# The second batch's split three units later in the dense layers, and the three products of a unit in another order

## The chip, the cores and the metric

One core of a Trainium2 chip. The metric is the time of one execution on the device in microseconds (us). Three runs of the kernel before took 1726.03, 1732.5 and 1733.97 us, median 1732.5.

## The reference, cut to what matters

```python
# x, v: (2, 12480, 128) f32
h_filt = (np.maximum(pos_emb @ w1, 0) @ w2) * np.exp(-0.01 * pos)[:, None]
y = irfft(rfft(x * v, n=2 * S, axis=1) * rfft(h_filt, n=2 * S, axis=0), n=2 * S, axis=1)[:, :S]
a = (x * y).reshape(24960, 128)              # a long convolution, gated by x
h = a @ w_in                                 # (24960, 2048)
g = np.maximum(h, 0) + alpha * np.minimum(h, 0)
out = (g @ w_out).astype(np.float32)         # (24960, 128)
```

## The kernel before, in words

The first third of the execution (to about 607 us) transforms the inputs and leaves the product of the spectra in DRAM (`g_d`). The change does not touch it. The rest is `phase_b`: the last stage of the inverse transform, the gate with x, and the two dense layers.

`phase_b` works in 32 **passes** (`k`, `NK = 32`). A pass covers 390 tokens of each of the two batches and walks over the 2048 hidden columns in 16 **units** (`f`, `NFT = 16`) of 128 columns. Numbers are kept in two fp16 halves, a high and a low one, so a product of two numbers is three matmuls: high by high, high by low, low by high. `mm3` (L1180) issues them, each for both batches, six matmuls a unit and layer.

The units overlap. In each step of the loop `for n in range(total + LAG)` (L1294) the program writes down, in this order:

- `layer1(n)`: six matmuls from the pass's input halves `ah` and `alo` into a PSUM tile `hp`, of which there are two in turn; ScalarE (ACT) takes `Relu(-h)` out of it (L1262), and VectorE (DVE) makes the activation from both (L1263, the op named `ring<-ring,keep,hp`). So unit n cannot start its matmuls before the L1263 of unit n-2 is done.
- `halve(n-1)`: ACT rounds the activation to fp16 (`g_hi`, L1269), and the rest (`g_lo`, L1270) is taken by DVE for even units, by GpSimd (POOL) for odd ones.
- `layer2(n-4)` (`LAG = 4`): six matmuls from `g_hi` and `g_lo` into `o`, the pass's output.
- one or two **steps of the next pass**, by a table that gives the step numbers for each unit: step 1 and 2 split the spectra of the first and the second batch into halves (`gh` on ACT, L1144, and `gl` on POOL, L1145); 3 and 5 are the last transform of either batch, 24 small matmuls into `yp` (L278 to L280); 4 and 6 the gate (DVE, L284); 7 the squares for the norm (ACT, L1160, and a cast on DVE); 8 their sum over partitions (one matmul, L1164); 9 the scales (five tiny DVE ops); 10 the halves `ah` (ACT, L1174) and `alo` (DVE, L1175) with which unit 0 of the next pass begins.

Each engine runs its instructions in the order in which they are written down; nothing reorders them. The table `usual` (L1292) holds for passes 1 to 30. Pass 0 has a table of its own, `late`, since its inputs come late, and pass 31 has no next pass to prepare. `late` has step 9 at unit 13 and step 10 at unit 14.

Of the kernel before, what the change touches and what calls it, by code (L numbers as in the profile page):

```python
# [49 lines left out]
LAG = 4  # L50
# [69 lines left out]
class Plan:  # L120
# [7 lines left out]
    LAG = {"PE": 200, "ACT": 150, "DVE": 110, "POOL": 110, "DMA": 1700, None: 0}  # L128
# [159 lines left out]
def body(ctx, tc, A, out, stop=None, dbg=None):  # L288
# [815 lines left out]
    with tc.manual_schedule():  # L1104
        ve.memset(ones, 1.0)
        ve.memset(one1, 1.0)
        with ExitStack() as ctx_a:
            xt = phase_a()
        if stop in ("p", "r"):
            return  # L1110
        if stop == "a":
            sy.dma_start(out=dbg["g"], in_=g_d)
            sy.dma_start(out=dbg["iu"], in_=s_u)
            sy.dma_start(out=dbg["ih"], in_=s_h)
            return
        phase_b(ctx, tc, A, out, locals())


def phase_b(ctx, tc, A, out, v):
# [58 lines left out]
        return st, norm, total, power, halves  # L1178

    def mm3(o, wh, wl, dh, dl, start, stop, bs=range(B)):  # L1180
        for n, (w, d) in enumerate(((wh, dh), (wh, dl), (wl, dh))):
            for b in bs:
                te.matmul(o[:, b, :TOK], w, d[:, b], start=start and n == 0, stop=stop and n == 2)  # L1183

# [52 lines left out]
    for n in range(NFT // 4):  # L1237
        c = n == 0 and FIRST
        w = sb.tile([128, 4 - c, 4, 128], F16, tag=f"w{n}", bufs=1, name="w")
# [15 lines left out]
    def layer1(n, d):  # L1255

        f = n % NFT
        hp = ps.tile([128, 2, 512], F32, tag="h", name="hp")
        mm3(hp, wt[0, f], wt[1, f], d["h"], d["l"], True, True)
        h = hp[:, :, :TOK]  # L1260
        neg, acts[n] = slot(n % 3), slot(3 + n % 3)
        ac.activation(neg, h, AF.Relu, scale=-1.0)  # L1262
        ve.scalar_tensor_tensor(out=acts[n], in0=neg, scalar=keep[:, f:f + 1], in1=h, op0=ALU.mult, op1=ALU.add)  # L1263
# [9 lines left out]
    def layer2(n):  # L1273
        k, f = divmod(n, NFT)
        if f == 0:
            outs[k] = ps.tile([128, 2, 512], F32, tag="o", bufs=1, name="o")
        d = parts.pop(n)
        split = n == total - 1
        for bs in [(b,) for b in range(B)] if split else [range(B)]:
            mm3(outs[k], wt[2, f], wt[3, f], *d, f == 0, f == NFT - 1, bs)  # L1280
        if f == NFT - 1:
            ot = sb.tile([D, B, TOK], F32, tag="ot", name="ot")
            for b in range(B):
                ac.activation(ot[:, b], outs[k][:, b, :TOK], AF.Copy, scale=backs[k][:, b:b + 1])  # L1284
                if split:
                    (sy, ac)[b].dma_start(out=out[k][:, b], in_=ot[:, b])
            if not split:
                sy.dma_start(out=out[k], in_=ot)
            outs.pop(k)


    usual = {0: [1], 2: [2], LAG: [3], LAG + 1: [4], 7: [5], 8: [6], 9: [7], 11: [8], 12: [9], 13: [10]}  # L1292
    late = {4: [1], 5: [2], 7: [3], 8: [4], 9: [5], 10: [6], 11: [7], 13: [8, 9], 14: [10]}
    for n in range(total + LAG):  # L1294
        k, f = divmod(n, NFT)
        if n < total:
            if f == 0:
                d = st["a"]
# [72 lines left out]
```

## Time and profile before

| | |
|---|---|
| median of three runs | 1732.5 us |
| the profiled execution, its own time | 1733.39 us |
| its span in the trace | 1731.5 us |
| PE (matmul) busy | 1616.6 us, 93% of the span |
| DVE busy | 1399.2 us, 81% |
| ACT busy | 1341.1 us, 77% |
| POOL busy | 968.8 us, 56% |
| dense layers, matmuls L1183 | from 612.6 us to the end |

The shares are means over both parts of the program. Times in the trace are counted from the start of the span. In a timeline a row is one instruction, or several alike in a row (x2); what stands in brackets is how long the engine was idle before it, and on whose result it waited.

### The profile page before, as it was taken

The page shows a single profiled execution, that of the slowest core. Times are in us where ns is not written, and L with a number is a line of the kernel's source. Part 1 is how long each engine was busy: PE and PEld are TensorE (multiplying, and loading weights), DVE is VectorE, ACT ScalarE, POOL GpSimd, SP SyncE. Part 2 cuts the span into 40 slices and gives each one's busy share as a digit, 9 for nine tenths or more (in the row PEclk, how much of TensorE's full clock was granted, in tenths as well). Part 3 has the DMA queues.
Part 4 walks back from the last instruction along what each step waited for, and adds up shares of the span by engine and source line. Part 5 has one row for each costly group of instructions (what it writes and reads, how often), then busy time and mean ns, then how long its engine had stood idle before and what let it go on. Part 6 is the DMA issues. An engine that isn't in the chain of part 4 may idle for free.

```text
span 1731.5 us, 34059 instructions
## 1 busy us (share of the span) xinstructions
PE 1616.6 (93%) x13260; PEld 1146.1 (66%) x13260; DVE 1399.2 (81%) x1931; ACT 1341.1 (77%) x2218; POOL 968.8 (56%) x687
## 2 busy tenths in 40 slices
PE   6988888888888989999999999999999999999998
PEld 4987877887778945665566556655665556555655
DVE  6566899986988778888888888888888888888886
ACT  6456677676786578888888888888888888888886
POOL 5356689777687145545554555445544554455443
PEclk8776898998999999999999999999999999999999
DMA  7142243675442960220221202202112022021100
GB/s 209 62 143 99 92 141 129 193 230 180 152 147 85 251 160 20 72 54 20 53 58 34 53 19 72 54 20 53 54 38 53 20 72 54 19 54 51 41 10 19
DMA packets 95568, 144.59 MB, mean 84 GB/s; under 512 B 7187, under 2 KB 63861, under 8 KB 93967
## 3 DMA queue, kind: packets, MB, share of 16 engines
q1 hardware_dynamic: 94287, 141.72, 28.0%
q8 instruction: 103, 1.69, 0.4%
q10 hardware_dynamic: 1120, 0.70, 0.1%
q14 instruction: 58, 0.48, 0.1%
HBM read 100.39 MB, written 42.01 MB: 82 GB/s over the span
## 4 chain that ended last, share of the span: by engine, by line
PE 62%; DVE 16%; ACT 9%; issue 6%; DMA 5%; POOL 2%; SPq 0%; POOLq 0%; ACTq 0%; DVEq 0%
PE hp L1183 24%; PE o L1183 22%; DVE ring L1263 4%; DVE ring L828 4%; PE mm L430 3%; ACT ring L1262 3%; DVE ring L838 3%; DMA g_d<-ring 2%; DMA first<-in_xv 2%; ACT g_hi L1269 2%; POOL ring L679 1%; PE yp L278 1%; PE yp L279 1%; PE yp L280 1%; DVE g_lo L1270 1%
## 5 line engine op out<-in xcount | busy, mean ns | idle before, releaser
L1183 PEld LDWEIGHTS <-w 128*128 128x128 f16 x6144 | 590.1, 97 | 444.0 <-issue 35.2
L1270 POOL TENSOR_TENSOR g_lo<-ring,g_hi 128x780 f16<-128x780 f32 x256 | 442.3, 1728 | 546.3 <-ACT g_hi L1269 546.2
L1263 DVE SCALAR_TENSOR_TENSOR ring<-ring,keep,hp 128x780 f32<-128x780 f32 x512 | 524.3, 1024 | 188.2 <-ACT ring L1262 181.4
L1262 ACT ACTIVATE ring<-hp 128x780 f32<-128x780 f32 x512 | 419.1, 819 | 169.1 <-PE hp L1183 167.6
L1183 PE MATMUL hp<-ah,w 128*128 128x390 f16 x2048 | 506.0, 328 | 15.1 <-DVE ring L1263 14.1
L1183 PE MATMUL o<-g_hi,w 128*128 128x390 f16 x2048 | 504.4, 328 | 0.7 <-ACT ot L1284 0.7
L1269 ACT ACTIVATE g_hi<-ring 128x780 f16<-128x780 f32 x512 | 433.8, 847 | 2.6 <-DVE ring L1263 0.3
L1270 DVE TENSOR_TENSOR g_lo<-ring,g_hi 128x780 f16<-128x780 f32 x256 | 330.4, 1291 | 0.0
L1183 PE MATMUL hp<-alo,w 128*128 128x390 f16 x1024 | 253.4, 328 | 0.8 <-DVE alo L1175 0.8
L1183 PE MATMUL o<-g_lo,w 128*128 128x390 f16 x1024 | 252.6, 328 | 0.6 <-POOL g_lo L1270 0.6
L1145 POOL TENSOR_TENSOR gl<-gt,gh 90x1024 f16<-90x1024 f32 x62 | 132.7, 2141 | 0.0
L828 DVE TENSOR_TENSOR ring<-mm,ring 128x512 f32<-128x512 f32 (+2 forms) x188 | 116.1, 657 | 17.3 <-ACT ring L816 16.4
L855 POOL TENSOR_TENSOR z<-ring,z 128x512 f16<-128x512 f32 x88 | 110.5, 1256 | 7.2 <-ACT z L851 7.2
L729 DVE TENSOR_TENSOR z<-mm,z 128x720 f16<-128x720 f32 (+1 forms) x99 | 85.6, 878 | 31.2 <-ACT z L726 31.1
L929 PE MATMUL mm<-t,z 128*128 128x128 f16 x512 | 102.5, 232 | 7.9 <-ACT z L851 3.8
L833 POOL TENSOR_TENSOR ring<-ring 128x256 f32<-128x256 f32 (+1 forms) x90 | 80.7, 897 | 48.1 <-DVE ring L828 39.8
L714 PE MATMUL mm<-t,ring 98*128 98x180 f16 (+1 forms) x320 | 83.5, 264 | 20.5 <-DVE z L729 5.3
L931 PE MATMUL mm<-t,z 128*128 128x128 f16 x512 | 101.8, 231 | 0.1
L930 PE MATMUL mm<-t,z 128*128 128x128 f16 x512 | 101.8, 231 | 0.0
L679 POOL TENSOR_TENSOR ring<-ring 98x512 f16<-98x512 f32 x63 | 78.9, 1267 | 39.0 <-ACT ring L676 25.5
L726 ACT ACTIVATE z<-mm 128x720 f16<-128x720 f32 (+1 forms) x99 | 74.4, 757 | 31.7 <-PE mm L716 31.1
L946 DVE TENSOR_TENSOR ring<-mm,ring 90x504 f32<-90x504 f32 (+2 forms) x132 | 80.5, 656 | 21.6 <-ACT ring L943 20.3
(177 smaller groups left out, 2939.4 us busy)
## 6 DMA issues: line engine op xcount, KB each, us to landing
g_d<-ring SPq DMA_DIRECT2D x32, 720.0 KB
gt<-g_d SPq DMA_DIRECT2D x16, 1440.0 KB
ring<-in_tw SPq DMA_DIRECT2D x34, 512.0 KB
ring<-in_xv SPq DMA_DIRECT2D x72, 196.0 KB
xt<-in_xt SPq DMA_DIRECT2D x31, 390.0 KB
out_t<-ot SPq DMA_DIRECT2D x31, 390.0 KB
first<-in_xv SPq DMA_DIRECT2D x56, 196.0 KB
first<-in_tw SPq DMA_DIRECT2D x12, 512.0 KB
```

Of the source, the lines that this page charges most:

```text
L679: either[e].tensor_tensor(out=halves(h)[:, 1], in0=xr(j), in1=halves(h)[:, 0], op=ALU.subtract)
L828: ve.tensor_tensor(out=t[:, :, m], in0=p[:, :, m], in1=hs[:, a:a + 1, m].to_broadcast([128, 2, (b1 - b0) * 2 * ZC]), op=ALU.mult)
L855: e.tensor_tensor(out=zl, in0=v, in1=zh, op=ALU.subtract)
L929: te.matmul(o, hi, t3[:, 0], start=True, stop=False)
L930: te.matmul(o, hi, t3[:, 1], start=False, stop=False)
L931: te.matmul(o, lo, t3[:, 0], start=False, stop=True)
L1145: po.tensor_tensor(out=dl, in0=src, in1=dh, op=ALU.subtract)
L1183: te.matmul(o[:, b, :TOK], w, d[:, b], start=start and n == 0, stop=stop and n == 2)
L1262: ac.activation(neg, h, AF.Relu, scale=-1.0)
L1263: ve.scalar_tensor_tensor(out=acts[n], in0=neg, scalar=keep[:, f:f + 1], in1=h, op0=ALU.mult, op1=ALU.add)
L1269: ac.activation(gh, a, AF.Copy)
L1270: (ve, po)[n % 2].tensor_tensor(out=gl, in0=a, in1=gh, op=ALU.subtract)
```

## The change

Two edits. In `mm3` the three products of a unit come in the order high by high, low weight by high data, high weight by low data; before, the product with the low data came second. `mm3` serves both layers. In the table `usual`, step 2 (the second batch's split) moves from unit 2 to unit 5, and steps 5 to 10 each move one unit later. The same instructions are issued, in equal numbers.

```diff
     def mm3(o, wh, wl, dh, dl, start, stop, bs=range(B)):
-        for n, (w, d) in enumerate(((wh, dh), (wh, dl), (wl, dh))):
+        for n, (w, d) in enumerate(((wh, dh), (wl, dh), (wh, dl))):
             for b in bs:
                 te.matmul(o[:, b, :TOK], w, d[:, b], start=start and n == 0, stop=stop and n == 2)
...
-    usual = {0: [1], 2: [2], LAG: [3], LAG + 1: [4], 7: [5], 8: [6], 9: [7], 11: [8], 12: [9], 13: [10]}
+    usual = {0: [1], LAG: [3], LAG + 1: [4, 2], 8: [5], 9: [6], 10: [7], 12: [8], 13: [9], 14: [10]}
     late = {4: [1], 5: [2], 7: [3], 8: [4], 9: [5], 10: [6], 11: [7], 13: [8, 9], 14: [10]}
```

The end of a pass on DVE, before: L1263 of unit 12, the five tiny ops of step 9 (L332 to L1170), L1263 of unit 13, `g_lo` of unit 12, the two `alo`, L1263 of units 14 and 15, and `g_lo` of unit 14.

```order
L1263 SCALAR_TENSOR_TENSOR ring<-ring,keep,hp 128x780
L332 TENSOR_SCALAR yp<-yp 128x2
L333 TENSOR_SCALAR yp<-yp 128x2
L334 TENSOR_SCALAR kap<-yp 128x2
L338 TENSOR_SCALAR yp<-kap 128x2
L1170 TENSOR_SCALAR osc<-yp,igsc 128x2
L1263 SCALAR_TENSOR_TENSOR ring<-ring,keep,hp 128x780
L1270 TENSOR_TENSOR g_lo<-ring,g_hi 128x780
L1175 SCALAR_TENSOR_TENSOR alo<-a,kap,ah 128x390 x2
L1263 SCALAR_TENSOR_TENSOR ring<-ring,keep,hp 128x780 x2
L1270 TENSOR_TENSOR g_lo<-ring,g_hi 128x780
```

The same place on DVE with the change: L1263 of units 12 and 13, `g_lo` of unit 12, the tiny ops, L1263 of unit 14, the two `alo`, L1263 of unit 15, `g_lo` of unit 14.

```order
L1263 SCALAR_TENSOR_TENSOR ring<-ring,keep,hp 128x780 x2
L1270 TENSOR_TENSOR g_lo<-ring,g_hi 128x780
L332 TENSOR_SCALAR yp<-yp 128x2
L333 TENSOR_SCALAR yp<-yp 128x2
L334 TENSOR_SCALAR kap<-yp 128x2
L338 TENSOR_SCALAR yp<-kap 128x2
L1170 TENSOR_SCALAR osc<-yp,igsc 128x2
L1263 SCALAR_TENSOR_TENSOR ring<-ring,keep,hp 128x780
L1175 SCALAR_TENSOR_TENSOR alo<-a,kap,ah 128x390 x2
L1263 SCALAR_TENSOR_TENSOR ring<-ring,keep,hp 128x780
L1270 TENSOR_TENSOR g_lo<-ring,g_hi 128x780
```

The tiny ops now stand behind the `g_lo` of unit 12, and the two `alo` stand behind the L1263 of unit 14 where they stood ahead of it.

The start of a pass on POOL, before: the seven odd `g_lo` that end with that of unit 15, the first batch's `gl`, `g_lo` of unit 1, the second batch's `gl`, the seven `g_lo` of units 3 to 15.

```order
L1270 TENSOR_TENSOR g_lo<-ring,g_hi 128x780 x7
L1145 TENSOR_TENSOR gl<-gt,gh 90x1024
L1270 TENSOR_TENSOR g_lo<-ring,g_hi 128x780
L1145 TENSOR_TENSOR gl<-gt,gh 90x1024
L1270 TENSOR_TENSOR g_lo<-ring,g_hi 128x780 x7
```

The same place on POOL with the change:

```order
L1270 TENSOR_TENSOR g_lo<-ring,g_hi 128x780 x6
L1145 TENSOR_TENSOR gl<-gt,gh 90x1024
L1270 TENSOR_TENSOR g_lo<-ring,g_hi 128x780 x2
L1145 TENSOR_TENSOR gl<-gt,gh 90x1024
L1270 TENSOR_TENSOR g_lo<-ring,g_hi 128x780 x6
```

The second `gl` has moved behind the `g_lo` of unit 3; the first one stands where it stood.

## Rows read from the trace of the kernel before

**Rows 1.** The page, busy time of each engine, its share of the span, instructions.

```profile
PE 1616.6 (93%) x13260; PEld 1146.1 (66%) x13260; DVE 1399.2 (81%) x1931; ACT 1341.1 (77%) x2218; POOL 968.8 (56%) x687
```

**Rows 2.** Busy time by window, passes 1 to 30: length, engines, clock, DMA.

```profile
660.00:1700.00 1040.00, 1027.17 (x7206) 620.95 (x7205) 864.31 (x1021) 881.18 (x1258) 535.54 (x298) 1.00 0.16 44
```

**Rows 3.** Waits from 640 to 1700 us: total us, times, longest.

```profile
PE hp L1183 <- DVE ring L1263: 12.6, 32, 0.4
PE hp L1183 <- DVE alo L1175: 0.8, 2, 0.6
```

**Rows 4.** Timeline of PE in an ordinary pass; unit 0 at 857.08.

```profile
839.96 0.21 PE L278 MATMUL yp<-t,gh 90*128 90x98 f16 x1
...
849.01 0.49 PE L1183 MATMUL hp<-ah,w 128*128 128x390 f16 x2
...
856.64 0.49 PE L1183 MATMUL o<-g_hi,w 128*128 128x390 f16 x2
857.08 0.49 PE L1183 MATMUL hp<-ah,w 128*128 128x390 f16 x2
...
864.71 0.49 PE L1183 MATMUL o<-g_hi,w 128*128 128x390 f16 x2
865.61 0.49 PE L1183 MATMUL hp<-ah,w 128*128 128x390 f16 x2 [0.40 <-DVE ring L1263]
```

**Rows 5.** Timeline of DVE in the same stretch.

```profile
837.03 0.96 DVE L1270 TENSOR_TENSOR g_lo<-ring,g_hi 128x780 f16<-128x780 f32 x1
...
838.45 1.02 DVE L1263 SCALAR_TENSOR_TENSOR ring<-ring,keep,hp 128x780 f32<-128x780 f32 x1
...
847.76 1.03 DVE L1263 SCALAR_TENSOR_TENSOR ring<-ring,keep,hp 128x780 f32<-128x780 f32 x1 [0.65 <-ACT ring L1262]
...
854.93 1.16 DVE L1175 SCALAR_TENSOR_TENSOR alo<-a,kap,ah 128x390 f16<-128x390 f32 x2
856.00 2.12 DVE L1263 SCALAR_TENSOR_TENSOR ring<-ring,keep,hp 128x780 f32<-128x780 f32 x2
...
862.52 2.10 DVE L1270 TENSOR_TENSOR g_lo<-ring,g_hi 128x780 f16<-128x780 f32 x1
864.54 2.04 DVE L1263 SCALAR_TENSOR_TENSOR ring<-ring,keep,hp 128x780 f32<-128x780 f32 x2
```

**Rows 6.** Timeline of ACT in the same stretch.

```profile
835.95 0.85 ACT L1269 ACTIVATE g_hi<-ring 128x780 f16<-128x780 f32 x1
...
859.79 1.05 ACT L1144 ACTIVATE gh<-gt 90x1024 f16<-90x1024 f32 x1
```

**Rows 7.** Timeline of POOL in the same stretch.

```profile
861.66 2.13 POOL L1145 TENSOR_TENSOR gl<-gt,gh 90x1024 f16<-90x1024 f32 x1
```

**Rows 8.** Timeline of PE where pass 1 begins, after pass 0's table `late`.

```profile
647.26 0.49 PE L1183 MATMUL o<-g_hi,w 128*128 128x390 f16 x2
647.60 0.49 PE L1183 MATMUL hp<-ah,w 128*128 128x390 f16 x2
648.66 0.33 PE L1183 MATMUL hp<-alo,w 128*128 128x390 f16 x1 [0.57 <-DVE alo L1175]
649.20 0.33 PE L1183 MATMUL hp<-alo,w 128*128 128x390 f16 x1 [0.21 <-DVE alo L1175]
649.36 0.49 PE L1183 MATMUL hp<-ah,w 128*128 128x390 f16 x2
649.69 0.49 PE L1183 MATMUL o<-g_hi,w 128*128 128x390 f16 x2
```

**Rows 9.** Timeline of DVE at that place.

```profile
646.50 1.02 DVE L1263 SCALAR_TENSOR_TENSOR ring<-ring,keep,hp 128x780 f32<-128x780 f32 x1
647.43 1.71 DVE L1175 SCALAR_TENSOR_TENSOR alo<-a,kap,ah 128x390 f16<-128x390 f32 x2
649.06 1.01 DVE L1263 SCALAR_TENSOR_TENSOR ring<-ring,keep,hp 128x780 f32<-128x780 f32 x1
```

**Rows 10.** Timeline of POOL at that place.

```profile
646.51 1.67 POOL L1270 TENSOR_TENSOR g_lo<-ring,g_hi 128x780 f16<-128x780 f32 x1 [1.69 <-ACT g_hi L1269]
```

## The prediction

> **What bounds the kernel now.** I read the page first: PE is busy 93% of the span, DVE 81%, ACT 77% [rows 1]. That is a mean over two unlike parts, so the second view is the busy time of the dense layers alone: in the 1040 us from 660 to 1700 PE is busy 1027.17 us at the full granted clock, DVE 864, ACT 881, POOL 536 [rows 2]. The stretch that the change touches is bound by matmuls, and all that can be won or lost there is a wait of PE. The third view lists those waits: PE waits for DVE's L1263 32 times, 12.6 us in all, and twice for `alo`, 0.8 us [rows 3]. The fourth, the timeline of PE, places them. Matmuls in an unbroken stream start 0.166 us apart, a pair of them 0.33 us (649.36 to 649.69, [rows 8]), so a pair that comes later than 0.33 us after the one before it shows a loss:
>
> - Unit 4: the pair at 864.71 should be followed at 865.04 and is followed at 865.61 [rows 4]. 0.57 us lost, in each of passes 1 to 30.
> - Unit 0: 856.64 is followed at 857.08 [rows 4], 0.44 where 0.33 is due. 0.11 us lost in each of passes 2 to 31.
>
> So a pass loses 0.68 us, 30 passes 20 us. No rearrangement of this kind can win more than these 20 us, and it can lose more.
>
> **What holds unit 4.** It needs the PSUM tile of unit 2, so the L1263 of unit 2. That one starts at 864.54 (the first of the x2 there) and takes 1.02 us: 865.56, then PE at 865.61 [rows 4, 5]. DVE was late with it because the `g_lo` of unit 0 ahead of it ran from 862.52 to 864.62, 2.10 us where the same op takes 0.96 us elsewhere in the pass (837.03) [rows 5]. Beside it POOL ran a `gl` from 861.66 to 863.79 [rows 7]: 863.79 + 0.96 = 864.75, so the DVE op did next to nothing until POOL was done. Which `gl`? The ACT op that feeds it is the `gh` at 859.79 [rows 6], in unit 0: it belongs to the first batch. The change leaves step 1 in unit 0. The second batch's `gl`, which does move, comes behind the `g_lo` of unit 1 on POOL and so after 863.79, when unit 4's fate is already decided. So I cost the removal of the second split from unit 2 at nothing: it frees DVE and ACT in units 3 and 4, and PE shows no wait there after 865.61 that could go. The 0.57 us stay.
>
> **What holds unit 0, and what the later steps do to it.** Before, the two `alo` run at 854.93 to 856.09, one whole unit before unit 0 needs them; the 0.11 us come from L1263 of unit 14, which they push to 856.00 + 1.02 = 857.02 [rows 4, 5]. With the change the tiny ops of step 9 stand at unit 13 and the `alo` at unit 14, behind the L1263 of that unit. This order exists in the trace already: the table `late` of pass 0 has steps 9 and 10 at the same units. There L1263 of unit 14 starts at 646.50, the two `alo` start at 647.43 and end at 649.14, 1.71 us for both instead of 1.16 [rows 5, 9]. The extra 0.55 us stands beside POOL's `g_lo` of unit 13, 646.51 to 648.18 [rows 10]; in the ordinary pass no such overlap falls on `alo`. PE starts the next pass's unit 0 on time at 647.60, but has its `alo` products only at 648.66 and 649.20, and layer 2 follows at 649.69 [rows 8]: 2.09 us for a unit of six matmuls that takes 1.00 us. 1.09 us lost.
>
> Each boundary of passes 1 to 30 should now look like that one: POOL's `g_lo` of unit 13 hangs on ACT and PE, and DVE's queue from `g_lo` of unit 12 to `alo` is the same in both. Step 8 comes one unit earlier than in `late`, which changes nothing, since in pass 0 DVE goes on to the tiny ops without a pause.
>
> The new order of products eases it. Four of the six matmuls now need only `ah`: they start at 647.60 to 648.10, the fifth would start at 648.26 and waits for 648.66, the sixth for 649.20, and layer 2 starts at 649.36. That is 649.36 - 647.60 - 1.00 = 0.76 us lost instead of 1.09.
>
> The Trainium skill, "SBUF — State Buffer", section "Who interferes with whom", says that a DVE op with two SBUF inputs and a GpSimd op that reads SBUF exclude each other, and that the second to issue is blocked until the first has finished. That agrees in kind with the rows. Taken to the letter, `alo` would begin at 648.18 and the pair would end at 649.34, not 649.14; the rows show 0.2 us less than the rule. By the rule the sum below would be 6 us higher; it is a rival at the end.
>
> **The sum.** A boundary costs 0.76 us where it cost 0.11: 0.65 us more, 30 times, 19.5 us. Pass 1's own beginning, still under `late`, gains 0.33 us from the order of products. In the very last unit one product fewer stands behind the last `g_lo`, 0.17 us. So 19.5 - 0.5 = 19.0 us on top of the profiled execution's 1733.4 us (span 1731.5): **1752 us**. That execution lies 0.9 us above the median of the three runs, which I leave as it is, since the runs themselves span 8 us.
>
> **Bounds of the pieces that the trace doesn't show.** For the `alo`: if the overlap with POOL did not fall on them, they would take 1.16 us from 647.43, to 648.59; the sixth matmul, due at 648.43, would start at 648.64, 0.21 us late, and the change would cost 0.10 x 30 = 3 us. At the other end is the full 0.96 us a boundary (0.76 + 0.20), 25 us. I take 0.76, the row at the same place of the program.
>
> For the second split at its new place: ACT does `gh` (1.05 us) behind the `g_hi` of unit 4, which ends at 835.95 + 0.85 = 836.80 [rows 6], so POOL's `gl` begins at about 837.85. DVE's `g_lo` of unit 4 starts at 837.03 and is done at 837.99 [rows 5]: it is there first. ACT's Relu of unit 6 ends at about 837.85 + 0.82 = 838.67, and L1263 of unit 6 at 839.7 instead of 839.47 [rows 5]. Unit 8 now comes ahead of the second transform and wants that tile at 839.96, where the transform began before [rows 4]: 0.2 us to spare. If DVE lost the port instead, its `g_lo` would end near 837.85 + 2.13 + 0.96 = 840.9, L1263 of unit 6 at 842.0 at the earliest, and unit 8 would wait 2 us a pass, 60 us in all. Cost taken: 0, the case in the rows, in which DVE's op starts 0.8 us ahead; bounds 0 and 60.
>
> For the norm: before, step 7 lets L1263 of unit 10 end at 847.76 + 1.03 = 848.79 [rows 5], and unit 12 starts at 849.01 [rows 4], 0.22 us to spare. With the change unit 11 and unit 13 stand there, with the same ops around them. Cost 0; each 0.1 us that is missing would cost 3 us.
>
> For the order of products elsewhere: weights are loaded for every matmul in either order, and a layer-2 unit needs its `g_lo` later than before. Nothing waits there now [rows 3]. Cost 0.
>
> **The rivals.**
>
> 1. The port does not hold up `alo`: POOL's `g_lo` of unit 13 falls elsewhere, since the earlier step 8 lets DVE be ahead. Then the new order hides most of it: 1733.4 + 3 - 0.5 = 1736 us, no change. For it: in passes 1 to 30 before, no `alo` was slowed. Against it: there the `alo` stood a unit earlier, and the one boundary with them at unit 14 shows the overlap. It decides if the `alo` start later than POOL's end or before its start. 7 in 100.
> 2. The moved split does free unit 4. If the wait there were in truth the second split's (through ACT or POOL), 0.57 x 30 = 17 us come back: 1735 us, no change, with `alo` as I say. Against it: the order of the starts above. 4 in 100. If, besides, `alo` costs no more than now, 1733.4 - 17 - 3 - 0.5 = 1713 us, faster. 4 in 100.
> 3. The full exclusion of the rule: 1758 us. 8 in 100.
> 4. A new wait at unit 8 or 13 from the thin margins: from 1760 us up to 1812 us (1752 + 60). 5 in 100.
> 5. The forecast, with the sum's own range of 1748 to 1756 us: 72 in 100.
>
> **How the numbers follow.** About 0.5% (8.7 us) is what a measurement of this kernel can tell from no change. Slower by more are the forecast and rivals 3 and 4: 0.85. Within it are rival 1 and the first half of rival 2: 0.11. Faster: 0.04. The range of 1744 to 1760 us holds the forecast and rival 3; outside stay the rivals below and the large waits, together 2 in 10.
>
> **What would show it right or wrong.** In the changed profile, unit 0 of each pass should show PE waiting for `alo` twice, some 0.8 us together as starts go, 30 times and once more in pass 1, and the `alo` pair should take about 1.7 us instead of 1.16. The wait for L1263 in unit 4 should stand as it is, with a `g_lo` of 2.1 us ahead of it; DVE's `g_lo` of unit 2, slowed by the second `gl` before, should be back near 0.96 us without PE gaining from it. A pass should take about 0.65 us longer. I am wrong if unit 4's wait is gone, if the `alo` run undisturbed, or if PE waits in unit 8 or 13.

## The result, and the profile after

The changed kernel takes 1753.39 us (median of 4 runs, 1750.11 to 1756.79) where the kernel before took 1732.72 us in the runs beside it (1726.03 to 1733.97): a ratio of 1.0127, 95% interval 1.0094 to 1.0161. It is slower by about 21 us. The forecast was 1752 us.

The dense layers are where the time went. In the window that [rows 2] shows for before, PE is busy 1013.61 us instead of 1027.17, still at the full granted clock (length of the window, then PE, PEld, DVE, ACT, POOL with instruction counts, clock, DMA):

```profile
660.00:1700.00 1040.00, 1013.61 (x7106) 609.89 (x7104) 826.91 (x996) 861.97 (x1233) 530.05 (x294) 1.00 0.16 44
```

The trace counts 100 matmuls fewer on PE in the same stretch. The waits of the changed kernel from 640 to 1720 us say at what (engine and line, whom it waited for, total us, times, longest):

```profile
PE hp L1183 <- DVE alo L1175: 15.6, 62, 0.3
...
PE hp L1183 <- DVE ring L1263: 12.2, 30, 0.4
```

Set against [rows 3]: PE's wait for L1263 at unit 4 is what it was, 12 us in 30 waits. The two more of before stood at unit 0 of two passes, at 822.40 and 1377.62 us, which began 0.38 us late, not 0.11 as the others. The wait for `alo`, which came twice in that stretch of before, now comes 62 times, two for each of 31 boundaries (a boundary is the place where one pass ends and the next begins). The timeline of PE around one of them, and the fifth unit after it (start, duration, operation, count, idle time before with its releaser):

```profile
826.26 0.49 PE L1183 MATMUL o<-g_lo,w 128*128 128x390 f16 x2
826.59 0.82 PE L1183 MATMUL hp<-ah,w 128*128 128x390 f16 x4
827.71 0.33 PE L1183 MATMUL hp<-alo,w 128*128 128x390 f16 x1 [0.30 <-DVE alo L1175]
828.25 0.33 PE L1183 MATMUL hp<-alo,w 128*128 128x390 f16 x1 [0.21 <-DVE alo L1175]
828.41 0.82 PE L1183 MATMUL o<-g_hi,w 128*128 128x390 f16 x4
...
835.05 0.49 PE L1183 MATMUL o<-g_lo,w 128*128 128x390 f16 x2
835.94 0.82 PE L1183 MATMUL hp<-ah,w 128*128 128x390 f16 x4 [0.40 <-DVE ring L1263]
```

Unit 0 starts on time (826.26 to 826.59 is the 0.33 us of a pair). Its four products with `ah` run through. The fifth, due at 827.25, comes at 827.71, the sixth at 828.25, and layer 2 follows at 828.41: 1.82 us where 1.00 is due. So 0.82 us are lost, read in starts as in [rows 8]; the brackets show less, since a matmul is drawn 0.33 us long in these rows although the next one starts 0.166 us after it. Unit 4 is 0.56 us late (due at 835.38), as in [rows 4].

The timeline of DVE at the same place:

```profile
825.41 1.02 DVE L1263 SCALAR_TENSOR_TENSOR ring<-ring,keep,hp 128x780 f32<-128x780 f32 x1
826.35 1.84 DVE L1175 SCALAR_TENSOR_TENSOR alo<-a,kap,ah 128x390 f16<-128x390 f32 x2
...
832.85 2.10 DVE L1270 TENSOR_TENSOR g_lo<-ring,g_hi 128x780 f16<-128x780 f32 x1
834.88 1.95 DVE L1263 SCALAR_TENSOR_TENSOR ring<-ring,keep,hp 128x780 f32<-128x780 f32 x2
836.81 0.97 DVE L1270 TENSOR_TENSOR g_lo<-ring,g_hi 128x780 f16<-128x780 f32 x1
...
846.02 1.43 DVE L1270 TENSOR_TENSOR g_lo<-ring,g_hi 128x780 f16<-128x780 f32 x1
```

And that of POOL:

```profile
825.56 1.67 POOL L1270 TENSOR_TENSOR g_lo<-ring,g_hi 128x780 f16<-128x780 f32 x1 [2.31 <-ACT g_hi L1269]
...
832.00 2.13 POOL L1145 TENSOR_TENSOR gl<-gt,gh 90x1024 f16<-90x1024 f32 x1
834.36 2.12 POOL L1270 TENSOR_TENSOR g_lo<-ring,g_hi 128x780 f16<-128x780 f32 x1 [0.23 <-ACT g_hi L1269]
```

The two `alo` take 1.84 us where they took 1.16 ([rows 5]), beside the `g_lo` of unit 13 on POOL that ends at 827.23. This is [rows 9, 10] again, now in every pass. The `g_lo` of unit 0 is still 2.10 us long beside the first batch's `gl` (832.00 to 834.13). The `g_lo` of unit 2, which the second `gl` had stretched to 2.56 us before (the line below), is back at 0.97 us, and PE gains nothing by it. The second `gl` now delays POOL's `g_lo` of unit 5 instead, beside which DVE's `g_lo` of unit 6 takes 1.43 us (846.02); PE doesn't wait for that either.

```profile
866.50 2.56 DVE L1270 TENSOR_TENSOR g_lo<-ring,g_hi 128x780 f16<-128x780 f32 x1
```

How long a pass takes is read off PE's start of unit 4 in passes 1 and 30, first in the kernel before, then in the changed one:

```profile
657.23 0.49 PE L1183 MATMUL hp<-ah,w 128*128 128x390 f16 x2 [0.40 <-DVE ring L1263]
1663.65 0.49 PE L1183 MATMUL hp<-ah,w 128*128 128x390 f16 x2 [0.41 <-DVE ring L1263]
658.90 0.49 PE L1183 MATMUL hp<-ah,w 128*128 128x390 f16 x2 [0.40 <-DVE ring L1263]
1685.69 0.49 PE L1183 MATMUL hp<-ah,w 128*128 128x390 f16 x2 [0.41 <-DVE ring L1263]
```

1006.42 us for 29 passes before, 1026.79 after: 34.70 and 35.41 us a pass, 0.70 us more, 21.1 us in 30 passes.

### The profile page after: what moved, and what is told of

It is laid out like the page before. It is cut to its first block, busy times and chain, and to the rows that moved or that the text cites. A ratio compares the mean times of both kernels' runs of the same rounds, so it can differ in the third digit from the quotient of the medians.

```text
span 1754.2 us, 34059 instructions
## 1 busy us (share of the span) xinstructions
PE 1624.3 (93%) x13260; PEld 1146.4 (65%) x13260; DVE 1379.8 (79%) x1931; ACT 1338.1 (76%) x2218; POOL 968.9 (55%) x687
## 4 chain that ended last, share of the span: by engine, by line
PE 54%; DVE 21%; ACT 11%; issue 6%; DMA 5%; POOL 2%; SPq 0%; ACTq 0%; POOLq 0%; DVEq 0%
PE hp L1183 21%; PE o L1183 18%; DVE ring L1263 6%; ACT ring L1262 4%; DVE ring L828 4%; DVE alo L1175 3%; PE mm L430 3%; DVE ring L838 3%; ACT g_hi L1269 3%; DMA g_d<-ring 2%; DMA first<-in_xv 2%; DVE g_lo L1270 1%; PE yp L278 1%; PE yp L279 1%; PE yp L280 1%
## 5 line engine op out<-in xcount | busy, mean ns | idle before, releaser
L1183 PEld LDWEIGHTS <-w 128*128 128x128 f16 x6144 | 590.2, 97 | 464.6 <-issue 58.2
L1263 DVE SCALAR_TENSOR_TENSOR ring<-ring,keep,hp 128x780 f32<-128x780 f32 x512 | 520.6, 1022 | 215.3 <-ACT ring L1262 213.1
L1183 PE MATMUL hp<-ah,w 128*128 128x390 f16 x2048 | 424.5, 329 | 14.2 <-DVE ring L1263 13.1
L1183 PE MATMUL o<-g_hi,w 128*128 128x390 f16 x2048 | 422.6, 328 | 0.7 <-ACT ot L1284 0.7
L1270 DVE TENSOR_TENSOR g_lo<-ring,g_hi 128x780 f16<-128x780 f32 x256 | 296.1, 1157 | 0.0
L1183 PE MATMUL hp<-alo,w 128*128 128x390 f16 x1024 | 257.9, 328 | 15.6 <-DVE alo L1175 15.6
L1183 PE MATMUL o<-g_lo,w 128*128 128x390 f16 x1024 | 252.6, 328 | 0.4 <-POOL g_lo L1270 0.4
```

The lines of the kernel that those rows point to most:

```text
L1270: (ve, po)[n % 2].tensor_tensor(out=gl, in0=a, in1=gh, op=ALU.subtract)
```

## The experiments

Two theories were set against each other. **The port** (the expectations' name for it: a DVE op with both tensors in SBUF and a POOL op hold each other up): the loss is step 10 at unit 14, whose `alo` are held until POOL is done with unit 13's `g_lo`, and unit 4's wait belongs to the first batch's split, which did not move. **Its rivals**: the order of products, the moved split, or a DVE queue that is merely longer ahead of `alo`.

### The order of products alone

```diff
-        for n, (w, d) in enumerate(((wh, dh), (wh, dl), (wl, dh))):
+        for n, (w, d) in enumerate(((wh, dh), (wl, dh), (wh, dl))):
```

> Only the order of the three products is changed, the table of steps is that of before. Theory (the loss is step 10 at unit 14, whose low halves wait for POOL): the order alone moves nothing in passes 2 to 31, gains 0.33 us once at pass 1 and some tenths at the end: 1732 us, ratio to before 0.998 to 1.002, unit 0 still 0.11 us late, unit 4 still 0.57 us late. Rival (the order itself costs, by more changes of weights): slower by up to the whole 21 us.

Measured: 1733.5 us against 1733.55 us, ratio 0.9996 (0.9982 to 1.0010). No difference, as the theory had it. In its trace unit 0 is 0.10 us late and unit 4 0.57 us, as before; unit 0 of pass 1 loses 0.76 us instead of 1.09, too little to see in the time. The new order costs nothing and gains nothing that the time shows by itself.

### The table alone

```diff
-    usual = {0: [1], 2: [2], LAG: [3], LAG + 1: [4], 7: [5], 8: [6], 9: [7], 11: [8], 12: [9], 13: [10]}
+    usual = {0: [1], LAG: [3], LAG + 1: [4, 2], 8: [5], 9: [6], 10: [7], 12: [8], 13: [9], 14: [10]}
```

> Only the table of steps is changed, the products keep their order of before. Theory: each of 30 boundaries loses what the boundary from pass 0 to 1 lost, 1.1 to 1.2 us where it lost 0.11, so 30 to 33 us more than before, 1763 us, and 10 us slower than the whole change, since the low data is wanted two matmuls earlier (0.33 us x 31). Rival (the order of products is what costs): as before, 1733 us.

Measured: 1765.35 us against 1733.55, ratio 1.0190 (1.0163 to 1.0217), 32 us slower, and by the two ratios 11 us worse than with both edits. The timeline of PE at a boundary:

```profile
825.85 0.49 PE L1183 MATMUL hp<-ah,w 128*128 128x390 f16 x2
826.97 0.33 PE L1183 MATMUL hp<-alo,w 128*128 128x390 f16 x1 [0.62 <-DVE alo L1175]
...
828.00 0.49 PE L1183 MATMUL o<-g_hi,w 128*128 128x390 f16 x2
```

Unit 0 takes 2.15 us here and 1.82 with the new order: two matmuls, 0.33 us, that now run ahead of the wait instead of behind it. The new order is a remedy, for a third of the harm that the table does.

### The second split alone

```diff
-    usual = {0: [1], 2: [2], LAG: [3], LAG + 1: [4], 7: [5], 8: [6], 9: [7], 11: [8], 12: [9], 13: [10]}
+    usual = {0: [1], LAG: [3], LAG + 1: [4, 2], 8: [5, 6], 9: [7], 11: [8], 12: [9], 13: [10]}
```

> Order of products as before; of the table only the second batch's split moves to unit 5, with its transform at unit 8 and its gate there too; norm, sum, scales and halves stay where they were before. Theory: unit 4's wait belongs to the first batch's split, so it stays at 0.57 us and the time is that of before, 1731 to 1736 us; VectorE's low part of unit 2 falls from 2.56 to 0.96 us without gain. Rival (the second split holds up unit 4): 17 us faster, 1716 us. Second rival (the moved split is what makes the change slow): 20 us slower, 1753 us.

Measured: 1734.3 us against 1733.55, ratio 1.0002 (0.9976 to 1.0028). The timeline of DVE from unit 0's `g_lo` to unit 2's:

```profile
858.79 2.10 DVE L1270 TENSOR_TENSOR g_lo<-ring,g_hi 128x780 f16<-128x780 f32 x1
860.82 1.95 DVE L1263 SCALAR_TENSOR_TENSOR ring<-ring,keep,hp 128x780 f32<-128x780 f32 x2
862.75 0.97 DVE L1270 TENSOR_TENSOR g_lo<-ring,g_hi 128x780 f16<-128x780 f32 x1
```

The second op has lost its stretch (0.97 us), the first has not (2.10 us), and PE waits behind the first alone. Moving the second split (and its transform one unit later) costs and gains nothing that the time shows: both rivals on it fall.

### Step 10 alone

```diff
-        for n, (w, d) in enumerate(((wh, dh), (wh, dl), (wl, dh))):
+        for n, (w, d) in enumerate(((wh, dh), (wl, dh), (wh, dl))):
...
-    usual = {0: [1], 2: [2], LAG: [3], LAG + 1: [4], 7: [5], 8: [6], 9: [7], 11: [8], 12: [9], 13: [10]}
+    usual = {0: [1], 2: [2], LAG: [3], LAG + 1: [4], 7: [5], 8: [6], 9: [7], 11: [8], 12: [9], 14: [10]}
```

> The new order of products, and of the table only step 10 (the halves) moves from unit 13 to 14; the split and all other steps stand as before. The scales are then ready a unit earlier than in the whole change. Theory (port shared with POOL): the two low halves start about 0.7 us earlier than in the whole change but are still held until POOL's low part of unit 13 is done, so unit 0 loses about 0.8 us all the same and the time is that of the whole change, 1750 to 1756 us. Rival (the halves are late because VectorE's queue ahead of them is long): they end 0.7 to 0.9 us earlier than in the whole change, unit 0 waits 0.1 us or less, and the time is 1728 to 1735 us.

Measured: 1754.92 us against 1733.55, ratio 1.0123 (1.0103 to 1.0142): the whole loss, from one step moved by one unit, with the new order of products. The timeline of DVE at a boundary:

```profile
825.61 1.03 DVE L1263 SCALAR_TENSOR_TENSOR ring<-ring,keep,hp 128x780 f32<-128x780 f32 x1 [0.21 <-issue]
826.56 2.11 DVE L1175 SCALAR_TENSOR_TENSOR alo<-a,kap,ah 128x390 f16<-128x390 f32 x2
```

POOL there:

```profile
826.04 1.67 POOL L1270 TENSOR_TENSOR g_lo<-ring,g_hi 128x780 f16<-128x780 f32 x1 [2.39 <-ACT g_hi L1269]
```

PE there:

```profile
827.07 0.82 PE L1183 MATMUL hp<-ah,w 128*128 128x390 f16 x4
828.18 0.33 PE L1183 MATMUL hp<-alo,w 128*128 128x390 f16 x1 [0.29 <-DVE alo L1175]
828.72 0.33 PE L1183 MATMUL hp<-alo,w 128*128 128x390 f16 x1 [0.21 <-DVE alo L1175]
828.88 0.82 PE L1183 MATMUL o<-g_hi,w 128*128 128x390 f16 x4
```

The `alo` start 0.51 us ahead of unit 0 here (826.56 against 827.07), 0.24 us ahead of it in the whole change. They end no earlier for it: they take 2.11 us instead of 1.84, and unit 0 takes 1.81 us instead of 1.82. Both ends lie at the same distance behind POOL's: 826.56 + 2.11 = 828.67 against 827.71, and 826.35 + 1.84 = 828.19 against 827.23, 0.96 us each. A queue that is merely shorter or longer would have moved the end. (I had expected a start 0.7 us earlier; it was 0.27. DVE is idle for 0.21 us ahead of the L1263 at 825.61, and the trace names no wait for it.) What costs time is thus not what the title of this document names, the second split's move, but one of the steps that move along with it: the halves, step 10.

### The whole change, with POOL out of the way

```diff
-        (ve, po)[n % 2].tensor_tensor(out=gl, in0=a, in1=gh, op=ALU.subtract)
+        (ve, po)[n % 2 if n % NFT not in (12, 13) else 1 - n % 2].tensor_tensor(out=gl, in0=a, in1=gh, op=ALU.subtract)
```

> The whole change, but the low parts of units 12 and 13 change engines: unit 12's is made by POOL, unit 13's by VectorE, so that POOL is through before the two low halves start, while VectorE has as many operations ahead of them as in the whole change. Theory (port shared with POOL): the low halves run undisturbed, 1.16 us for both instead of 1.77; unit 0 waits for the second alone, 0.2 to 0.4 us instead of 0.82, so 13 to 18 us of the loss come back: 1735 to 1740 us. Rival (VectorE's queue): no change against the whole change, 1750 to 1756 us.

Measured: 1742.13 us against 1734.09 in the runs beside it, ratio 1.0047 (1.0029 to 1.0065): 8 us over the kernel before instead of 21. The timeline of DVE at a boundary:

```profile
858.43 0.96 DVE L1270 TENSOR_TENSOR g_lo<-ring,g_hi 128x780 f16<-128x780 f32 x1
859.31 1.16 DVE L1175 SCALAR_TENSOR_TENSOR alo<-a,kap,ah 128x390 f16<-128x390 f32 x2
```

POOL there, the `g_lo` of unit 12 and then that of unit 15:

```profile
856.15 1.67 POOL L1270 TENSOR_TENSOR g_lo<-ring,g_hi 128x780 f16<-128x780 f32 x1 [0.18 <-ACT g_hi L1269]
862.58 1.67 POOL L1270 TENSOR_TENSOR g_lo<-ring,g_hi 128x780 f16<-128x780 f32 x1 [4.76 <-ACT g_hi L1269]
```

PE there:

```profile
859.29 0.82 PE L1183 MATMUL hp<-ah,w 128*128 128x390 f16 x4
859.99 0.33 PE L1183 MATMUL hp<-alo,w 128*128 128x390 f16 x1
860.52 0.33 PE L1183 MATMUL hp<-alo,w 128*128 128x390 f16 x1 [0.21 <-DVE alo L1175]
860.69 0.82 PE L1183 MATMUL o<-g_hi,w 128*128 128x390 f16 x4
```

With POOL's op done at 857.82, the `alo` take their 1.16 us, and unit 0 takes 1.40 us instead of 1.82: 0.42 us a boundary come back, 13 us in 30. They come back although the `alo` start later than in the whole change, 0.02 us behind unit 0 (859.31 against 859.29) where they started 0.24 us ahead of it (826.35 against 826.59), since unit 13's `g_lo` now stands right before them on DVE. By these rows 0.26 of the 0.40 us that are still lost here would be the price of the swap itself, and some 0.14 us would be left of the 0.82 without POOL; that is worked out and wasn't run. The wait is in the range given for it (0.40), the time 2 us above its own.

### The first split later

```diff
-    usual = {0: [1], 2: [2], LAG: [3], LAG + 1: [4], 7: [5], 8: [6], 9: [7], 11: [8], 12: [9], 13: [10]}
+    usual = {1: [1], 3: [2], LAG: [3], LAG + 1: [4], 7: [5], 8: [6], 9: [7], 11: [8], 12: [9], 13: [10]}
```

> The kernel before, with the first batch's split one unit later (unit 1) and the second's too (unit 3); everything else as before. Theory: VectorE's low part of unit 0 no longer meets a split on POOL (0.96 us instead of 2.10), the wait of unit 4 goes, and the 30 ordinary passes take 34.1 us instead of 34.7: 15 to 17 us faster than before, 1716 us. Against it: the low part of unit 1 stands behind the moved split on POOL and may come too late for layer 2, or another unit waits instead; then 1725 us to no gain at all. Rival (unit 4 is not held by the first split): the wait stays, 1733 us.

The edit moves both splits by one unit; that moving the second one gains nothing is known from its own experiment above.

Measured: 1718.25 us against 1734.09, ratio 0.9889 (0.9843 to 0.9935): faster than both kernels, by 16 us than the one before. Three of the four runs took 1718 to 1721 us, one 1702.61. The timeline of DVE, the `g_lo` of unit 0 and L1263 of unit 2:

```profile
860.44 0.96 DVE L1270 TENSOR_TENSOR g_lo<-ring,g_hi 128x780 f16<-128x780 f32 x1
861.96 1.03 DVE L1263 SCALAR_TENSOR_TENSOR ring<-ring,keep,hp 128x780 f32<-128x780 f32 x1 [0.55 <-ACT ring L1262]
```

POOL there, the first batch's `gl`:

```profile
861.23 2.17 POOL L1145 TENSOR_TENSOR gl<-gt,gh 90x1024 f16<-90x1024 f32 x1 [1.20 <-ACT gh L1144]
```

PE at units 0 and 4:

```profile
854.96 0.49 PE L1183 MATMUL o<-g_hi,w 128*128 128x390 f16 x2
855.40 0.49 PE L1183 MATMUL hp<-ah,w 128*128 128x390 f16 x2
...
863.03 0.49 PE L1183 MATMUL o<-g_hi,w 128*128 128x390 f16 x2
863.37 0.49 PE L1183 MATMUL hp<-ah,w 128*128 128x390 f16 x2
```

DVE's `g_lo` of unit 0 starts ahead of the first `gl` now and takes 0.96 us; L1263 of unit 2 ends at 862.99, and unit 4 follows at its due time (863.03 to 863.37). In the window from 660 to 1690 us only 2 of PE's waits for L1263 are left, 0.4 us in all, and PE is busy 1028.89 of 1030 us:

```profile
660.00:1690.00 1030.00, 1028.89 (x7254) 624.88 (x7251) 816.65 (x1025) 886.85 (x1266) 527.32 (x301) 1.00 0.16 44
```

The 16 us agree with the 30 x 0.57 = 17 us of unit 4's wait, which thus belongs to the first batch's split. What is left is the 0.1 us at unit 0 (854.96 to 855.40).

## Why the prediction was right

- **PE is the bound, and only its waits count.** Right. The 21.1 us by which 30 passes grew are PE's waits at unit 0, and the last experiment got back what PE waited at unit 4. How busy DVE and ACT are does not decide it: in the same window both are busy less than before, in part because less of the work falls into it.
- **The second split's move is worth nothing.** Right: `g_lo` of unit 2 fell from 2.56 to 0.97 us, and the kernel with that move alone measured 1.0002. That `g_lo` of unit 6 would be stretched in its place (1.43 us) was not foreseen; it costs PE nothing.
- **Unit 4's 0.57 us stay, being the first split's.** Right: 0.56 us after, and gone when the first split moves.
- **A boundary becomes like that from pass 0 to pass 1.** Right in kind, a little small in size. Unit 0 lost 0.82 us where 0.76 was taken, because POOL's `g_lo` of unit 13 starts 1.03 us ahead of unit 0 in an ordinary pass (825.56 against 826.59) and 1.09 us ahead in pass 0 (646.51 against 647.60, [rows 8, 10]); the `alo` end with it, so they end 0.06 us later against PE. The 0.11 us taken for unit 0 before were a little small as well, since two of the passes lost 0.38. Together that is 0.70 us a pass against the forecast 0.65. With it the sum is 1733.4 + 21.1 - 0.5 = 1754.0 us; the changed kernel's profiled execution took 1756.8 us. Of the remaining 2.8 us, 1.9 lie ahead of the dense layers, whose first L1183 starts at 614.48 instead of 612.62 us, and 0.7 outside the traced span (1756.79 against 1754.2 us, before 1733.39 against 1731.5). The change leaves the part ahead of the dense layers alone; in the eight traces of this case their start lies between 609.17 and 614.72 us.
- **The number.** That 1752 us lies within 1.4 us of the median is in part luck: the runs of the changed kernel span 6.7 us, and the 19.5 us that the sum put on 30 passes were 21.1.
- **The new order of products gives back 0.33 us a boundary.** Right: 2.15 against 1.82 us.
- **The thin margins at units 8 and 13 hold.** Right; from 640 to 1720 us PE waits for L1263 at unit 4 alone. DVE's `g_lo` of unit 4 starts at 842.04, POOL's second `gl` at 842.83, as far apart as reckoned.
- **Rival 3, the `alo` begin only when POOL is done (1758 us).** Not quite: the pair ends 0.96 us behind POOL's end, where 1.16 us would follow a start at that end. The rows of before had shown the same 0.2 us, and the sum by rows came nearer.
- **The bound without the overlap (0.21 us lost at unit 0).** Not measured by itself: the swap leaves 0.40 us, of which 0.26 are reckoned to be its own doing.
- **Rival 2, its second half (1713 us).** Wrongly added up: if the `alo` cost no more than now, the 0.11 us at unit 0 stay, and the 3 us for them are not to be taken off: 1716 us.

## What to carry to other kernels

In a stretch that is bound by one engine, count only that engine's waits, and follow each back to the one instruction that held it: of two splits that looked alike, one cost 16 us and the other nothing. When a step moves to another place, look for a place in the trace where it already stands so; the first pass had its own table and showed the price of the new one to within 10%. Before an op with two SBUF operands on VectorE, ask what GpSimd is doing at that time.

## What the runs showed of the hardware

In these traces a VectorE op with both tensors in SBUF that starts well ahead of the end of a GpSimd op ends only behind that one: the `g_lo` of 0.96 us took 2.10 and ended 0.82 us behind (834.95 against 834.13), and the `alo` pair of 1.16 us took 1.84 or 2.11 depending on how early it was issued, with an end 0.96 us behind. It goes the other way too: GpSimd's `g_lo` that starts at 834.36, while VectorE's runs until 834.95, takes 2.12 us where others take 1.67. L1263, which reads one of its tensors from PSUM, ran through in 1.01 to 1.03 us in all these stretches. VectorE's op is through sooner after GpSimd's end than its own duration, the pair by 0.2 us in three kernels alike (before, the whole change, step 10 alone), the single `g_lo` by 0.14 us. The runs show that the two hold each other up; what in the chip they share, no run here shows.
